# Attention through memory slots and a max-out FFN on one core: a new written-out order of the pieces behind the first 92

## The chip, the cores and the metric

The kernel runs on one core of one Trainium2 chip. A core has five engines that work side by side, each through its own instructions in order: TensorE (PE, with its weight loads PEld), VectorE (DVE), ScalarE (ACT), GpSimd (POOL) and SyncE (SP, which here only issues stores). They meet through semaphores. Tensors lie in SBUF, matmul results in the eight banks of PSUM, inputs and the output in HBM. The metric is the device time of one execution in microseconds (us), the median of several runs; lower is better.

## What is computed

For each of 8 batches, 8 heads and 576 positions, phi gives 32 memory slots whose softmax over the positions gathers keys and values; the queries attend to the 32 slots; the result goes through a max-out FFN.

```python
a = exp(phi - max(phi, axis=2)); a = a / sum(a, axis=2)      # over the 576 positions
k_m = einsum('bhsm,bhsd->bhmd', a, k); v_m = einsum('bhsm,bhsd->bhmd', a, v)
attn = softmax(q @ k_m.T / 8)                                # over the 32 slots
x = (attn @ v_m) as rows of 512                              # 8 heads x 64, 4608 rows
out = max(x @ w1, x @ w2, x @ w3) @ w_out                    # 512 -> 768 -> 512
```

## The kernel before

The kernel never forms `x`. It folds the memory values of a batch into the FFN's weights (`fold`, the D pieces), so that the attention weights `attn` multiply folded weights directly. The max over three products is taken as h = max(relu(x(w1-w3)), x(w2-w3)) plus a term x w3 that goes straight into the output product through w3 times w_out. So the first FFN stage has two weights for each of six column tiles of 128, and the second stage adds two matmuls on `attn` with the folded `wp3`.

The work is cut into 402 pieces, and a string near the end of the kernel (lines 758 to 785) writes out their order by hand. A word such as `F6@2` is piece F6 of batch 2; `issue` (line 722) emits all its instructions, in program order, to the engines that they need. There is no planner at run time: the order of the words is the order in each engine's queue, and each engine takes its own instructions strictly in that order. A mark `!` moves one instruction of the piece to another engine (an eviction from ScalarE to VectorE or back, a sum or copy between VectorE, ScalarE and GpSimd). A second string (lines 144 to 146) gives the PSUM banks in the order in which the pieces ask for them; a piece waits until the last reader of its bank is done.

The pieces that the text speaks of:

- L0 loads phi (`load_ph`, line 94), L1 and L2 load k and v into the raw buffers `kvo` (line 98), L3 loads q (line 113). All are issued from GpSimd's queue, which also carries computing; two buffers each.
- r0 and r1 (`pack`, lines 106 and 108) copy the loaded k and v of a batch into the packed buffer `kvr`, on GpSimd or, with the mark, on ScalarE. They free the raw buffer for the load two batches on.
- E (line 232) is the exponential of phi on ScalarE. B (line 250) gathers keys and values, 72 small matmuls. N (lines 270 to 285) normalises them on VectorE, K (line 300) transposes them on TensorE, with an eviction.
- Q0, Q1 (line 315) transpose q on VectorE. S (line 335) makes the scores, with two exponentials on ScalarE (line 344).
- The softmax of a batch, for its two halves 0 and 1: a (line 389, transpose), s (397, sum), c (406, reciprocal) on VectorE, m (411, multiplication) on GpSimd, X (419, transpose back into `attn`) on VectorE.
- D0 to D3 (line 442) fold the values into the weights, with an eviction of about 1 us.
- F0 to F11 (line 468) are the first FFN stage, four matmuls of 288 columns each; the even ones are evicted with a relu into `h1`, the odd ones by VectorE's max with `h1` into `hT` (line 481).
- T0 to T4 (lines 658 to 676) are the second FFN stage for 128 rows each, with an eviction and a store.
- Batches 5 and 6 do the second stage with seven block products in place of eight (P0 to P6, line 600), as Strassen's scheme does. Their sums of blocks are the pieces U (of weights) and A (of activations), all at line 505. These have two operands in SBUF and run on GpSimd or VectorE:

```python
def combine(on_dve, out_, in0, in1, op):
    eng = nc.vector if on_dve else nc.gpsimd
    eng.tensor_tensor(out=out_, in0=in0, in1=in1, op=op)
```

For U the mark `!` means VectorE, for A it means GpSimd.

The functions that matter for the change, with the line numbers of the profile:

Of the kernel before, what the change touches and what calls it, by code (L numbers as in the profile page):

```python
# [15 lines left out]
def kernel(  # L16
# [14 lines left out]
    B, H, S, D = q.shape  # L31
# [104 lines left out]
    for i in range(P // M):  # L136
# [4 lines left out]
    banks = iter(  # L141
        "".join(
            """
            00232204420145545045024602460260426042672643424260246024604260462342656204502406
            24062046204267240670462064260246024602064326247420640642064024620462042604605264
            620502645264034063460406064026042640246204203406767676
            """.split()
        )
    )
# [606 lines left out]


    for w in """
        E@0 H2@0 H0@0 L3@0 Z25@0 B0@0 Y2@0 I@0 N0@0 Z2@0 K0@0! Q0@0 Q1@0 Z9@0 S@0 Z2@0
        M0@0 M1@0 R0@0 R1@0 W0@0 Y3@0 W1@0 W2@0 Z6@0 O1@0 H3@0 O3@0 O2@0 H1@0 X1@0 B1@0  # L760
        X0@0 N1@0 K1@0 O0@0 Y0@0 D1@0! D0@0! D3@0 F8@0 F10@0 F2@0 V0@0 F6@0 F0@0! Y1@0
        D2@0 D4@0 F4@0 L0@1 V1@0 F1@0 E@1 F3@0 L1@1 F5@0 F9@0 F7@0 L3@1 F11@0 B0@1 T3@0
        N0@1 K0@1! L2@1 Q1@1 L2@2 L1@2 Q0@1 L0@2 V2@0 T0@0! L3@2 S@1 T1@0 a0@1 s0@1 c0@1
        m0@1 B1@1 N1@1 a1@1 L1@3 K1@1 s1@1 D0@1 D1@1! D2@1 c1@1 m1@1 X0@1 L3@3 r1@2 X1@1
        T2@0! L2@3 F6@1 F10@1 F7@1 F2@1 F3@1 F4@1 F0@1 r0@2 E@2 F5@1 F1@1 F11@1 L0@3
        L0@4 F8@1 L2@4 F9@1 B@2 D3@1 N@2 Q1@2 T0@1! K@2 T2@1! r0@3 Q0@2 S@2 a0@2 a1@2
        s1@2 c1@2 m1@2 T4@1! D1@2! s0@2 D2@2 c0@2 m0@2 X1@2 D0@2 T3@1 Q0@3 L3@4 X0@2
        Q1@3 T1@1 F0@2 F4@2 F8@2 F6@2 F9@2 E@3 F7@2 F1@2 L1@4 r1@3 F10@2 F2@2 L2@5 B@3
        N@3 D3@2 F3@2 L1@5 F5@2 K@3! U0@9 F11@2 S@3 U1@9 E@4 T3@2 L0@5 T0@2! a1@3 D1@3!
        s1@3 D2@3 a0@3 r1@4 c1@3 L3@5 D0@3 T1@2 m1@3 s0@3 Q0@4 X1@3 c0@3 m0@3 X0@3 T2@2!  # L770
        F4@3! r0@4 F5@3 L2@6 F0@3 D3@3 B@4 F6@3 N@4 F1@3 F8@3 Q1@4 F2@3 F9@3 K@4! F10@3
        r1@5 F7@3 S@4 F11@3 L3@6 D3@4 E@5 r0@5 F3@3 a0@4 U3@9 L0@6 a1@4 T4@3! L1@6 L0@7
        s1@4 D0@4 D1@4! B@5 c1@4 N@5 T1@3 Q1@5 K@5 L1@7 Q0@5 s0@4 c0@4 m0@4 T3@3! S@5
        a0@5 T2@3! s0@5 a1@5 c0@5 X0@4 m1@4 X1@4 D2@4 D0@5 D1@5 m0@5 s1@5 X0@5 T0@3!
        F4@4 c1@5 F2@4 m1@5 r1@6 L2@7 F10@4 r0@6 F3@4 F5@4 F8@4 X1@5 F9@4 F0@4 F11@4
        F6@4 E@6 F10@5! F7@4 L3@7 F0@5 F2@5 A4@5! Q0@6 A5@5! F1@4 F1@5 A7@5! F8@5 F6@5
        F4@5! Q1@6 D3@5 B@6 N@6 r0@7 D2@5 T0@4! F7@5 F5@5 K@6 F3@5 U2@9 F9@5 U0@5! T1@4!
        F11@5 A0@5 A6@5 r1@7! E@7 S@6 T2@4! D1@6! U1@5! D2@6 a0@6 Q1@7 B@7 A1@5! U2@5
        U3@5 N@7 T3@4 s0@6 K@7! Q0@7 a1@6 P1@5 D3@6 s1@6 c1@6 S@7 c0@6 A2@5! m1@6 P2@5
        P4@5 a0@7 s0@7 D3@7 D2@7 m0@6 a1@7 c0@7 D1@7! P0@5! A3@5! U0@6 s1@7 P5@5 c1@7  # L780
        m1@7 X1@6 X0@6 T4@5! D0@6! D0@7 P6@5 U1@6 m0@7 F8@6 F9@6 F6@6 U3@6 U2@6 X0@7
        P3@5 F10@6 F2@6 X1@7 F11@6 F8@7 F0@6 F3@6 F7@6 F4@7 F1@6 F9@7 F4@6 A4@6 F5@6
        F2@7 F0@7 F5@7 A0@6! A6@6! A1@6! F6@7 F10@7! F3@7 A5@6! P1@6 A2@6! F1@7 P0@6
        F7@7 A3@6! F11@7 P2@6! P4@6 T0@7 T1@7 P5@6! A7@6 T4@7 P6@6! P3@6! T2@7! T3@7
    """.split():
        n, b = w.rstrip("!").split("@")
        issue(int(b), n, w.endswith("!"))
# [30 lines left out]
```

## Time and profile before

| quantity | value |
|---|---|
| median of three runs | 163.83 us (163.65 to 164.19) |
| profiled execution, whole | 164.42 us |
| its span, first to last instruction | 162.4 us, 4946 instructions |
| TensorE busy | 152.6 us (94%), 2128 matmuls |
| VectorE busy | 104.5 us (64%) |
| ScalarE busy | 97.8 us (60%) |
| GpSimd busy | 92.2 us (57%) |
| loads on GpSimd's queue | 21.43 MB, 69.1% of 16 engines' span |
| stores on SyncE's queue | 9.90 MB, 17.3% |

Mean durations of the instructions that the text counts with, from the profile's groups: one F matmul 286 ns (they overlap), VectorE's max of an odd F 752 ns, ScalarE's relu 657 ns, eviction of a D piece 996 ns on ScalarE and 1211 on VectorE, the exponential of scores 653 ns each, transpose a 468 ns, sum s 740 ns, reciprocal c 246 ns, multiplication m 1154 ns, transpose X 456 ns, copy r 2111 ns, transpose Q 760 ns, a sum U or A on GpSimd 670 or 1640 ns by its size. A load of q, k or v takes 14 to 17 us from its issue to landing, because several are under way.

How to read a row of the timeline: start in us from the span's start, duration of the merged run of instructions, engine, line of the kernel, operation, output <- inputs, shapes, count, and in brackets the engine's idle time before it with what ended it. A row of the windows has the stretch, its length, and for PE, PEld, DVE, ACT and POOL the busy time and the instructions; then the granted clock, the DMA's busy share and GB/s. A busy TensorE isn't TensorE at its peak, since matmuls are pipelined; the starts of successive pieces tell more.

### The profile page before, as it was taken

What the parts mean: (1) busy time and instruction counts of PE and PEld (TensorE: products, weight loads), DVE (VectorE), ACT (ScalarE), POOL (GpSimd) and SP (SyncE); (2) the same over time, 40 slices, a digit from 0 to 9 for tenths busy, and PEclk for the clock granted to TensorE, in tenths of its full rate; (3) what the DMA queues carried; (4) which work ended last, traced back from release to release, by engine and by line L of the source; (5) the groups of instructions that cost most, each with busy time, mean ns of one, the idle gap of its engine ahead of it and who ended that gap; (6) DMA issues with size and microseconds to landing.
All of it is one profiled execution on the core that took longest, in us unless ns stands there. A gap on an engine that the chain in (4) does not pass through costs nothing.

```text
span 162.4 us, 4946 instructions
## 1 busy us (share of the span) xinstructions
PE 152.6 (94%) x2128; PEld 90.5 (56%) x2128; DVE 104.5 (64%) x201; ACT 97.8 (60%) x144; POOL 92.2 (57%) x92
## 2 busy tenths in 40 slices
PE   7958798999798999999999999999999999999991
PEld 2433544673366535753584536776456577785570
DVE  2013703898837847577487797986999967874340
ACT  4204535934497468977689849688779786631110
POOL 7931115100598359899877964999094880395000
PEclk9999999999999999999999999999999999999999
DMA  5999999999999999999999999999221044000365
GB/s 153 152 205 208 206 211 214 276 208 210 250 323 232 212 244 378 261 237 205 261 318 230 212 312 306 286 183 174 84 96 65 4 164 160 4 0 0 129 253 199
DMA packets 21909, 31.76 MB, mean 196 GB/s; under 512 B 1152, under 2 KB 16512, under 8 KB 21888
## 3 DMA queue, kind: packets, MB, share of 16 engines
q0 software_dynamic: 16080, 21.43, 69.1%
q1 hardware_dynamic: 5664, 9.90, 17.3%
q8 instruction: 16, 0.26, 0.6%
q10 hardware_dynamic: 144, 0.13, 0.2%
q14 instruction: 5, 0.04, 0.1%
HBM read 39.32 MB, written 9.44 MB: 300 GB/s over the span
## 4 chain that ended last, share of the span: by engine, by line
PE 62%; DMA 27%; DVE 4%; POOL 3%; ACT 1%; issue 1%; POOLq 0%
PE psum L468 22%; PE psum L658 17%; DMA ph<-in_phi_dram 15%; DMA w_sb<-in_moe_w_dram 12%; PE psum L600 8%; PE psum L667 5%; PE psum L442 4%; PE psum L250 2%; POOL kvo L98 2%; PE psum L676 1%; PE psum L335 1%; DVE twb L505 1%; PE psum L699 1%; ACT e L232 1%; PE psum L300 1%
## 5 line engine op out<-in xcount | busy, mean ns | idle before, releaser
L468 PE MATMUL psum<-attn,wp 128*128 128x288 bf16 x384 | 50.2, 286 | 0.2
L468 PEld LDWEIGHTS <-wp 128*128 128x128 bf16 x384 | 36.9, 98 | 12.0 <-issue 1.5
L481 DVE TENSOR_TENSOR hT<-psum,h 128x576 bf16<-128x576 f32 x48 | 34.5, 752 | 12.7 <-PE psum L468 8.3
L658 PE MATMUL psum<-wo_sb,hT 128*128 128x512 bf16 x162 | 39.6, 380 | 0.0
L173 ACT ACTIVATE h<-psum 128x576 bf16<-128x576 f32 x43 | 26.1, 657 | 7.2 <-PE psum L468 7.1
L175 ACT CAST wp<-psum 128x1024 bf16<-128x1024 f32 (+1 forms) x30 | 28.4, 996 | 2.6 <-PE psum L442 2.6
L175 ACT COPY ot<-psum 128x512 f32<-128x512 f32 x23 | 13.6, 591 | 23.2 <-PE psum L667 18.2
L411 POOL TENSOR_TENSOR t<-t,sm 128x576 bf16<-128x576 bf16 x14 | 16.1, 1154 | 19.2 <-DVE sm L406 19.2
L108 POOL COPY kvr<-kvo 128x2304 bf16<-128x2304 bf16 x11 | 23.2, 2111 | 5.5 <-DMA kvo<-in_k_dram 4.4
L658 PEld LDWEIGHTS <-hT 128*128 128x128 bf16 x162 | 14.6, 98 | 17.8 <-issue 3.2
L667 PE MATMUL psum<-wp,attn 128*128 128x512 bf16 x46 | 13.7, 379 | 0.0
L344 ACT ACTIVATE e<-psum 128x576 bf16<-128x576 f32 x16 | 9.6, 653 | 6.1 <-PE psum L335 6.1
L162 PE MATMUL psum<-warm 128*128 128x512 bf16 x44 | 12.1, 428 | 1.2 <-DVE warm L131 1.2
L315 DVE STREAM_TRANSPOSE qT<-qq 128x576 f32<-128x576 f32 x16 | 12.0, 760 | 1.1 <-DMA qq<-in_q_dram 1.0
L232 ACT ACTIVATE e<-ph 128x1152 bf16<-128x1152 f32 (+1 forms) x9 | 9.5, 1061 | 2.9 <-DMA ph<-in_phi_dram 2.7
L98 POOL DMA_DIRECT2D kvo<-in_v_dram x9 | 6.8, 753 | 7.4 <-PE psum L250 4.1
L397 DVE TENSOR_REDUCE sm<-t 128x18 f32<-128x576 bf16 x14 | 10.4, 740 | 0.2
L113 POOL DMA_DIRECT2D qq<-in_q_dram x8 | 6.1, 759 | 6.3 <-DMA w_sb<-in_moe_w_dram 6.0
L250 PEld LDWEIGHTS <-e 64*32 64x32 bf16 x720 | 7.1, 90 | 4.5 <-issue 2.8
L389 DVE STREAM_TRANSPOSE t<-e 128x288 f32<-128x288 f32 x14 | 6.5, 468 | 4.0 <-ACT e L344 4.0
L98 POOL DMA_DIRECT2D kvo<-in_k_dram x9 | 6.9, 769 | 2.9 <-DMA qq<-in_q_dram 2.1
L419 DVE STREAM_TRANSPOSE attn<-t 128x288 f32<-128x288 f32 x14 | 6.2, 456 | 3.5 <-POOL t L411 3.5
(94 smaller groups left out, 181.0 us busy)
## 6 DMA issues: line engine op xcount, KB each, us to landing
out_dram<-ot SPq DMA_DIRECT2D x27, 256.0 KB, 6.0
qq<-in_q_dram POOLq DMA_DIRECT2D x8, 576.0 KB, 14.0
ph<-in_phi_dram POOLq DMA_DIRECT2D x7, 576.0 KB, 16.0
kvo<-in_k_dram POOLq DMA_DIRECT2D x7, 576.0 KB, 15.9
kvo<-in_v_dram POOLq DMA_DIRECT2D x7, 576.0 KB, 16.7
w_sb<-in_moe_w_dram POOLq DMA_DIRECT2D x3, 768.0 KB, 19.4
out_dram<-oj SPq DMA_DIRECT2D x4, 512.0 KB, 2.8
wo_sb<-in_moe_w_out_dram POOLq DMA_DIRECT2D x1, 768.0 KB, 15.0
```

The lines of the kernel that those rows point to most:

```text
L98: nc.gpsimd.dma_start(out=kv[:, i, h].rearrange("p j c d -> p j (c d)"), in_=by_pair((k, v)[i], b)[:, h],)
L108: nc.gpsimd.tensor_copy(out=out_, in_=in_)
L162: nc.tensor.matmul(po[:, 0:BANK], lhsT=warm[:, 0:P], rhs=warm, start=True, stop=True)
L173: nc.scalar.activation(out=out_, in_=in_, func=AF.Relu)
L175: nc.scalar.copy(out=out_, in_=in_)
L315: nc.vector.transpose(out=s["qT"][:, j].rearrange("p j c r e -> p (j c r e)").bitcast(FP32), in_=loaded[b]["q"][:, j].rearrange("p j c d - ...
L411: (nc.vector if swap else nc.gpsimd).tensor_tensor(out=t, in0=t, in1=s["sm", g].unsqueeze(2).to_broadcast([P, S // HP, R, 2]), op=ALU.mult,)
L468: nc.tensor.matmul(acc[:, h, 0:SH], lhsT=wps[b][:, g, w * DF + ft * P : w * DF + (ft + 1) * P], rhs=attn[:, g, c0 : c0 + SH], start=(g == ...
L481: nc.vector.tensor_tensor(out=hT[:, ft, (b % 2) * S : (b % 2 + 1) * S].rearrange("p (h n) -> p h n", h=2), in0=a, in1=s["h1", ft], op=ALU.max,
L600: nc.tensor.matmul(po[:, q * CH : (q + 1) * CH], lhsT=lhs(k, q), rhs=rhs(k), start=(i < 3 and k == 0 and q == 0), stop=(k == KT and q == 1 ...
L658: nc.tensor.matmul(po, lhsT=hT[:, fc, c0 : c0 + P], rhs=wo_sb[:, fc, :], start=(n == 0), stop=False,)
L667: nc.tensor.matmul(po, lhsT=attn[:, g, c0 : c0 + P], rhs=wp3s[b][:, g, :], start=False, stop=(g == NG - 1),)
```

## The change

Only the two strings change. The first 92 words of the order (to `X0@1`) and the first 60 banks stay. All other words are put in a new order: the same 402 pieces, so the same matmuls, loads, copies and stores, but other places in each engine's queue. 42 of them change the mark, so that an instruction of theirs changes engine. Behind the 92, VectorE gets 161 instructions (155 before), ScalarE 101 (110) and GpSimd 48 (45, loads not counted). Of the sums at line 505, VectorE had U0@5, A0@5, A6@5, U1@5, A4@6 and A7@6; it now has U2@9, U3@6, A7@6 and A2@6. The copy r1@7 moves from ScalarE to GpSimd.

```diff
--- before.py
+++ after.py
@@ -141,9 +141,9 @@
     banks = iter(
         "".join(
             """
-            00232204420145545045024602460260426042672643424260246024604260462342656204502406
-            24062046204267240670462064260246024602064326247420640642064024620462042604605264
-            620502645264034063460406064026042640246204203406767676
+            00232204420145545045024602460260426042672643424260246024604206420142656204502460
+            42642064024606421042064026420620426050624265042124604204624062406204602460246206
+            241042616202641064216416462624264206240642604304101323
             """.split()
         )
     )
@@ -761,27 +761,27 @@
         X0@0 N1@0 K1@0 O0@0 Y0@0 D1@0! D0@0! D3@0 F8@0 F10@0 F2@0 V0@0 F6@0 F0@0! Y1@0
         D2@0 D4@0 F4@0 L0@1 V1@0 F1@0 E@1 F3@0 L1@1 F5@0 F9@0 F7@0 L3@1 F11@0 B0@1 T3@0
         N0@1 K0@1! L2@1 Q1@1 L2@2 L1@2 Q0@1 L0@2 V2@0 T0@0! L3@2 S@1 T1@0 a0@1 s0@1 c0@1
-        m0@1 B1@1 N1@1 a1@1 L1@3 K1@1 s1@1 D0@1 D1@1! D2@1 c1@1 m1@1 X0@1 L3@3 r1@2 X1@1
-        T2@0! L2@3 F6@1 F10@1 F7@1 F2@1 F3@1 F4@1 F0@1 r0@2 E@2 F5@1 F1@1 F11@1 L0@3
-        L0@4 F8@1 L2@4 F9@1 B@2 D3@1 N@2 Q1@2 T0@1! K@2 T2@1! r0@3 Q0@2 S@2 a0@2 a1@2
-        s1@2 c1@2 m1@2 T4@1! D1@2! s0@2 D2@2 c0@2 m0@2 X1@2 D0@2 T3@1 Q0@3 L3@4 X0@2
-        Q1@3 T1@1 F0@2 F4@2 F8@2 F6@2 F9@2 E@3 F7@2 F1@2 L1@4 r1@3 F10@2 F2@2 L2@5 B@3
-        N@3 D3@2 F3@2 L1@5 F5@2 K@3! U0@9 F11@2 S@3 U1@9 E@4 T3@2 L0@5 T0@2! a1@3 D1@3!
-        s1@3 D2@3 a0@3 r1@4 c1@3 L3@5 D0@3 T1@2 m1@3 s0@3 Q0@4 X1@3 c0@3 m0@3 X0@3 T2@2!
-        F4@3! r0@4 F5@3 L2@6 F0@3 D3@3 B@4 F6@3 N@4 F1@3 F8@3 Q1@4 F2@3 F9@3 K@4! F10@3
-        r1@5 F7@3 S@4 F11@3 L3@6 D3@4 E@5 r0@5 F3@3 a0@4 U3@9 L0@6 a1@4 T4@3! L1@6 L0@7
-        s1@4 D0@4 D1@4! B@5 c1@4 N@5 T1@3 Q1@5 K@5 L1@7 Q0@5 s0@4 c0@4 m0@4 T3@3! S@5
-        a0@5 T2@3! s0@5 a1@5 c0@5 X0@4 m1@4 X1@4 D2@4 D0@5 D1@5 m0@5 s1@5 X0@5 T0@3!
-        F4@4 c1@5 F2@4 m1@5 r1@6 L2@7 F10@4 r0@6 F3@4 F5@4 F8@4 X1@5 F9@4 F0@4 F11@4
-        F6@4 E@6 F10@5! F7@4 L3@7 F0@5 F2@5 A4@5! Q0@6 A5@5! F1@4 F1@5 A7@5! F8@5 F6@5
-        F4@5! Q1@6 D3@5 B@6 N@6 r0@7 D2@5 T0@4! F7@5 F5@5 K@6 F3@5 U2@9 F9@5 U0@5! T1@4!
-        F11@5 A0@5 A6@5 r1@7! E@7 S@6 T2@4! D1@6! U1@5! D2@6 a0@6 Q1@7 B@7 A1@5! U2@5
-        U3@5 N@7 T3@4 s0@6 K@7! Q0@7 a1@6 P1@5 D3@6 s1@6 c1@6 S@7 c0@6 A2@5! m1@6 P2@5
-        P4@5 a0@7 s0@7 D3@7 D2@7 m0@6 a1@7 c0@7 D1@7! P0@5! A3@5! U0@6 s1@7 P5@5 c1@7
-        m1@7 X1@6 X0@6 T4@5! D0@6! D0@7 P6@5 U1@6 m0@7 F8@6 F9@6 F6@6 U3@6 U2@6 X0@7
-        P3@5 F10@6 F2@6 X1@7 F11@6 F8@7 F0@6 F3@6 F7@6 F4@7 F1@6 F9@7 F4@6 A4@6 F5@6
-        F2@7 F0@7 F5@7 A0@6! A6@6! A1@6! F6@7 F10@7! F3@7 A5@6! P1@6 A2@6! F1@7 P0@6
-        F7@7 A3@6! F11@7 P2@6! P4@6 T0@7 T1@7 P5@6! A7@6 T4@7 P6@6! P3@6! T2@7! T3@7
+        m0@1 B1@1 N1@1 a1@1 L1@3 K1@1 s1@1 D0@1 D1@1! D2@1 c1@1 m1@1 X0@1 T2@0! X1@1
+        F2@1 F10@1! F8@1! L2@3 F0@1! F9@1 F6@1 r1@2 F11@1 F4@1 r0@2 F3@1 F1@1 L0@3 F7@1
+        E@2 L3@3 L1@4 F5@1 B@2 D3@1 N@2 U2@9! Q1@2 Q0@2 T1@1! K@2! T3@1 r0@3 S@2 a0@2
+        s0@2 L2@4 r1@3 a1@2 c0@2 s1@2 m0@2 T4@1 c1@2 D3@2 D1@2! D0@2 m1@2 X0@2 E@3 T0@1
+        T2@1! D2@2 B@3 X1@2 F6@2 N@3 F2@2 Q0@3 L0@4 F7@2 K@3! L3@4 F10@2 F8@2 Q1@3 L1@5
+        F3@2 F9@2 L2@5 F0@2 F11@2 F4@2 L0@5 F1@2 F5@2 L3@5 S@3 T3@2 a0@3 a1@3 s0@3 s1@3
+        c1@3 r0@4 c0@3 r1@4 D1@3! D0@3! m0@3 m1@3 L2@6 E@4 D2@3! X0@3 U0@9 U1@9 T2@2!
+        X1@3 T0@2! D3@3 B@4 N@4 F2@3 F4@3 F0@3 Q0@4 F8@3! F6@3 F9@3 F1@3 L0@6 K@4! r0@5
+        Q1@4 F10@3 F7@3 F11@3 F5@3 T1@2! S@4 F3@3 a0@4 E@5 T2@3 r1@5 D3@4 L1@6 a1@4 D2@4
+        B@5 T0@3! N@5 L2@7 D0@4 Q0@5 D1@4! U3@9 s0@4 Q1@5 K@5 L0@7 s1@4 T1@3 S@5 c0@4
+        c1@4 T3@3 L1@7 D0@5 a0@5 s0@5 m1@4 m0@4 a1@5 c0@5 X1@4 D1@5! X0@4 D3@5 s1@5 m0@5
+        T4@3 c1@5 F2@4 F10@4 r1@6 X0@5 F3@4 F6@4 F8@4 F7@4 L3@6 E@6 F11@4 F4@4 m1@5 r0@6
+        X1@5 r1@7 L3@7 F0@4 F9@4 A4@5! F5@4 F6@5 D2@5 B@6 F8@5 N@6 F10@5 U0@5 F9@5 r0@7
+        F2@5 F1@4 K@6! F3@5 F11@5 F0@5 E@7 F7@5 F4@5 F5@5 Q1@6 T2@4 D1@6! D0@6 B@7 T1@4
+        N@7 Q0@6 K@7! U2@5 Q0@7 F1@5 S@6 T0@4! U1@5 Q1@7 A5@5! a1@6 a0@6 S@7 a0@7 s0@6
+        T4@5! c0@6 A0@5! A1@5! A7@5! D3@6 A6@5! D0@7 U3@5 D3@7! s1@6 c1@6 m0@6 m1@6 a1@7
+        s1@7 T3@4 X1@6 P1@5 A2@5! X0@6 c1@7 D1@7! D2@7 D2@6 P2@5 m1@7 P4@5! F8@6 F0@6
+        s0@7 c0@7 P0@5! F2@6! P5@5 F6@6 F7@6 m0@7 F4@6 X0@7 U0@6 A4@6! X1@7 P6@5 F3@6
+        F9@6 A3@5! A5@6! F2@7! P3@5! U2@6 F10@6 F1@6 F11@6 F8@7 F4@7 A6@6! F5@6 F3@7
+        F6@7 F0@7! A0@6! F10@7! F9@7 P1@6 F7@7 F1@7 F11@7 P0@6! P2@6 F5@7 A1@6! U1@6
+        P4@6 A3@6! T4@7 U3@6! A7@6 A2@6 T0@7! P3@6! P5@6 T1@7 P6@6 T2@7! T3@7
     """.split():
         n, b = w.rstrip("!").split("@")
         issue(int(b), n, w.endswith("!"))
```

## The prediction, made before the changed kernel ran

> **What bounds the kernel now.** I read four views: the page's head, the busy time by window, the timeline by engine, and the DMA rows (single loads with their landing, and the packets of each queue). The first fence holds the page's head and one window, from the first matmul of the first moved tensor piece (T2@0) to that of the last piece (T3@7).
>
> ```profile
> span 162.4 us, 4946 instructions
> ...
> 44.28:157.08 112.80, 112.16 (x1498) 69.48 (x1491) 82.54 (x156) 77.33 (x111) 76.64 (x66) 1.00 0.79 189
> ```
>
> In those 112.80 us TensorE is busy for 112.16, at full clock; VectorE, ScalarE and GpSimd are each busy for 77 to 83. TensorE is the bound, the block products are the same, and a new order can only win what TensorE waits. Busy time hides short waits (matmuls overlap), so I went by starts, from TensorE's rows of the timeline (the first row is ScalarE's).
>
> ```profile
> 51.36 1.16 ACT L232 ACTIVATE e<-ph 128x1152 bf16<-128x1152 f32 x1 [1.01 <-DMA ph<-in_phi_dram]
> 52.58 0.80 PE L250 MATMUL psum<-kvr,e 64*32 64x129 bf16 x72 [0.52 <-ACT e L232]
> 57.26 0.47 PE L335 MATMUL psum<-qT,kvt 32*32 32x288 bf16 x32
> 61.70 0.59 PE L667 MATMUL psum<-wp,attn 128*128 128x512 bf16 x2
> 62.13 1.46 PE L658 MATMUL psum<-wo_sb,hT 128*128 128x512 bf16 x6
> 63.43 0.59 PE L667 MATMUL psum<-wp,attn 128*128 128x512 bf16 x2
> 63.93 0.53 PE L468 MATMUL psum<-attn,wp 128*128 128x288 bf16 x3
> 70.39 0.33 PE L300 MATMUL psum<-ident,kvn 128*128 128x128 bf16 x3
> 70.56 0.65 PE L468 MATMUL psum<-attn,wp 128*128 128x288 bf16 x4
> 71.28 0.48 PE L335 MATMUL psum<-qT,kvt 32*32 32x288 bf16 x32
> 79.06 0.59 PE L667 MATMUL psum<-wp,attn 128*128 128x512 bf16 x2
> 79.61 0.65 PE L468 MATMUL psum<-attn,wp 128*128 128x288 bf16 x4
> 89.67 0.63 PE L442 MATMUL psum<-w_sb,kvt 64*32 64x512 bf16 x16
> 90.11 0.83 PE L250 MATMUL psum<-kvr,e 64*32 64x129 bf16 x72
> 90.87 0.39 PE L658 MATMUL psum<-wo_sb,hT 128*128 128x512 bf16 x1
> 115.58 0.65 PE L468 MATMUL psum<-attn,wp 128*128 128x288 bf16 x4
> 116.16 0.47 PE L335 MATMUL psum<-qT,kvt 32*32 32x288 bf16 x32
> 121.34 0.55 PE L300 MATMUL psum<-ident,kvn 128*128 128x128 bf16 x3
> 121.72 0.49 PE L600 MATMUL psum<-wo_sb,hT 128*128 128x256 bf16 x3
> ```
>
> An F piece to an S piece takes 0.58 us where nothing is late (115.58 to 116.16), but 0.72 at S@3 (70.56 to 71.28): 0.14 lost. A K piece takes 0.17 (70.39 to 70.56), K@7 0.38 (121.34 to 121.72): 0.21. The last two matmuls of a T piece take 0.43 (61.70 to 62.13), but 0.50 ahead of F0@2 (63.43 to 63.93) and 0.55 ahead of F4@3 (79.06 to 79.61): 0.07 and 0.12. The largest wait, 0.52 at B@2, stands on a load: the exponential E@2 (51.36) started when phi of batch 2 had landed, and B@2 behind it.
>
> **The change part by part.** *What is kept.* The first 92 pieces and the issue of that phi load are untouched, and ahead of B@2 stand T2@0 and the same twelve F pieces in both orders. B@2 stays at 52.58 and its 0.52 stays. The end of the order is P6@6, T2@7, T3@7 where it was P3@6, T2@7, T3@7, so the output queue ends alike: 0.
>
> *What can be won.* The four small waits: 0.14 + 0.21 + 0.07 + 0.12 = 0.54 us. TensorE also pays some 0.09 (0.58 against 0.49 for an F piece) at a switch between whole and partial tiles; of these the new order has 39, the old 41, but five B pieces, not three, are followed by a whole tile. I take 0, between -0.19 and +0.1.
>
> *The two-operand instructions.* They stand on VectorE at L505. This fence is VectorE's and GpSimd's timeline around the one case where they met.
>
> ```profile
> 115.41 0.28 DVE L505 TENSOR_TENSOR twb<-wp 128x256 bf16<-128x256 bf16 x1
> 117.81 1.64 POOL L505 TENSOR_TENSOR w_sb<-w_sb,hT 128x768 bf16<-128x768 bf16 x1 [4.52 <-DVE w_sb L505]
> 117.84 1.75 DVE L505 TENSOR_TENSOR twb<-wp,twb 128x256 bf16<-128x256 bf16 x1
> ```
>
> U1@5 needs 0.28 us like its sister at 115.41, but takes 1.75 and ends 0.14 behind GpSimd's 1.64: 1.47 us of VectorE lost. What it cost TensorE is K@7's 0.21, since N@7 stood behind it on VectorE; the rest was hidden. The new order has four such instructions (U2@9, U3@6, A7@6, A2@6) for six. At U2@9 (about 55 us) GpSimd waits for a load, and at the other three (about 149 us) its last combination, A3@6, is over: no cost, and the gain is inside the 0.54.
>
> *The order on GpSimd, which is where I expect the price.* Its timeline in the old order, then the landing of the loads issued at 45.60 (q of batch 3) and 48.45 (v), each from the row of its line.
>
> ```profile
> 45.60 0.81 POOL L113 DMA_DIRECT2D qq<-in_q_dram  x1
> 48.45 0.74 POOL L98 DMA_DIRECT2D kvo<-in_v_dram  x1
> 57.64 2.11 POOL L108 COPY kvr<-kvo 128x2304 bf16<-128x2304 bf16 x1 [3.31 <-DMA kvo<-in_k_dram]
> 61.09 2.27 POOL L411 TENSOR_TENSOR t<-t,sm 128x576 bf16<-128x576 bf16 x2 [1.34 <-DVE sm L406]
> 65.17 2.10 POOL L108 COPY kvr<-kvo 128x2304 bf16<-128x2304 bf16 x1 [0.32 <-DMA kvo<-in_v_dram]
> 63.40 0.48 DVE L419 STREAM_TRANSPOSE attn<-t 128x288 f32<-128x288 f32 x1
> ...
> DMA to landing us min/median/max: 15.3/15.3/15.3
> DMA to landing us min/median/max: 16.7/16.7/16.7
> ```
>
> The loads land in order of issue: k of batch 3 at 57.6, which ends the wait of r0@3 (57.64), q at 60.9, v at 65.1: slots of 3.3 and 4.2 us. In the old order the multiplications m1@2 and m0@2 (61.09) stood ahead of r1@3, the copy that waits for v of batch 3 (65.17). In the new one L2@4 and r1@3 stand ahead of m0@2 and m1@2, and v is issued right behind k. Queued behind the waiting r1@3 on GpSimd are m0@2 and m1@2, behind them on VectorE X0@2, T0@1's eviction and X1@2, and on TensorE F6@2.
>
> The sum: v takes q's slot and lands at 60.9; r1@3 60.95 to 63.06; the two multiplications 2.27, to 65.28; X1@2 0.48, to 65.8; F6@2's third matmul, which reads X1@2's half, at 65.85. Without a wait it would start at 65.15: S@2 at 57.2 as before; S, T4, three D and two T took 6.6 us (57.26 to 63.93, less 0.07); one D more is 0.22 (two from 89.67 to 90.11), B 0.76 (90.11 to 90.87), one switch more 0.09, two matmuls 0.25. Price 0.68. The lower end is 0.23: r1@3 can't start ahead of 60.45, when r0@3 (57.64 + 2.11) and L2@4 (0.74) are through. The upper end goes by v's own 4.2 us: 61.8, so 1.6. I take 0.68, the slot of a load of the same size at the same place.
>
> Outputs decide which slot it is. The rows below are the DMA answers for 54 to 58 us (the loads' queue, and the one output issued then) and for 60 to 64 us.
>
> ```profile
> q0 software_dynamic: 730, 0.81, 119.7%
> out_dram<-ot SPq DMA_DIRECT2D x1, 256.0 KB, 6.5
> ...
> q0 software_dynamic: 346, 1.03, 75.3%
> q1 hardware_dynamic: 253, 0.46, 31.8%
> ```
>
> With outputs (q1) in flight the loads move 346 packets in 4 us, without them 730. In the new order the outputs of T1@1 and T3@1 are issued at about 57.3 and 58.0, inside v's slot. Were they served at once, v would move at half speed from 58 on and land near 62. The old order's output, issued at 56.13, had no packet by 58.0 (54 to 58 lists no q1), so by this row they begin near 60 and v keeps the short slot.
>
> The Trainium skill ("DMA: Bandwidth & Descriptors", section "Queues, rings and completion order") says that a DMA engine takes turns between the rings that have work, a packet at a time; by that they would be served at once, and the sum would be the first rival's. The trace agrees with the sharing and not with its early start.
>
> *The next load, behind this.* The load of phi of batch 5, and E@5, which reads it:
>
> ```profile
> L94 POOL DMA_DIRECT2D ph<-in_phi_dram x1: 787/787/787, 72.4 to 72.4; - x1
> DMA to landing us min/median/max: 16.1/16.1/16.1
> ...
> 88.50 1.16 ACT L232 ACTIVATE e<-ph 128x1152 bf16<-128x1152 f32 x1
> ```
>
> E@5 started as its load landed (72.4 + 16.1 = 88.5). The same set of loads goes ahead of it in the new order, so E@5 again ends near 89.66. But B@5 (90.11) comes earlier: from S@2 TensorE needed 90.11 - 57.26 - 0.33 of waits = 32.5 us; the new order has a T4 and a D less and, net, no other piece changed save one T more (-0.4): 89.3. So B@5 would wait 0.4 if F6@2 hadn't; with the 0.68 it is covered. Each covers the other, so no less than 0.4 of the 0.54 is given back.
>
> *VectorE's queue.* Three evictions of F in a row on its timeline:
>
> ```profile
> 66.65 2.09 DVE L481 TENSOR_TENSOR hT<-psum,h 128x576 bf16<-128x576 f32 x3 [2.11 <-PE psum L468]
> ```
>
> They take 0.7 us each; TensorE makes an F in 0.49. Where a bank comes back after 1.47 to 1.64 us (F1@2 to T3@2, F9@3 to F7@3, F9@5 to F3@5, F2@5 among them) I find 0 to 0.1 us of room; I charge 0.18 in all, between 0 and 0.7 (one eviction late).
>
> Sum: -0.54 + 0 + 0.68 + 0.18 = +0.32 us. The profiled execution had 162.4 us of span and 164.42 in all, 0.59 above the runs' median of 163.83. I put the 0.32 on that median: 164.15, in the profiled terms 162.7 and 164.7.
>
> **The rivals.** *Loads come late (slower).* The outputs take half the DMA from 58 on, v lands near 62, F6@2 loses 1.7 us, and the copy r1@4, again ahead of m0@3 and m1@3, may repeat it at F2@3: 163.83 - 0.54 + 1.7 + 0.18 = 165.2. It decides from a landing of 61.1 on, where the sum passes +0.5. For it speaks v's 4.2 us slot; against it, the output that began late. It is also what the page's rule gives. *VectorE falls behind (slower).* D0@3 and D2@3 are evicted on VectorE between S@3 and X0@3. By the means in the table above, S@3's start to X1@3's end is 1.8 for the exponentials, 0.5 for the second transpose, 1.5 for two sums, 0.5 for two reciprocals, 2.4 for the evictions and 0.9 for two X: 7.6 us. The matmul that needs it stands 7.8 behind S@3 (three T 5.2, four D 0.9, B 0.8, S 0.4, two matmuls 0.25, switches 0.2). One eviction more (0.67) and a bank late elsewhere give +0.9: 164.7. *A real gain (faster).* If v lands by 60.4 and E@5's load by 88.1, the waits are 0.23 and no more: 163.83 - 0.54 + 0.23 - 0.19 = 163.3. Against it stands E@5's row. *It doesn't do what it says:* if U2@9 meets a GpSimd copy it takes up to 2.1 us, and S@2, with 0.7 of room, loses 1.4: 165.5. GpSimd's 3.31 us wait at that place speaks against it.
>
> **How the numbers follow.** Forecast 0.50, loads late 0.27, VectorE behind 0.10, not as said 0.05, real gain 0.08. 0.3% of 163.83 is 0.49 us, about what a measurement of this kernel can tell. So faster 0.08, same 0.50, slower 0.42. The forecast's own range is 163.7 to 164.4 (prices 0.4 to 0.9); the range of 8 in 10 goes up to the late loads, 163.5 to 165.2.
>
> **What would show it.** Right: GpSimd idle ahead of L108 at about 59.7, ended by v's load; F6@2 about 65.6, 0.7 behind its place; K@7 back at 0.17; all L505 on VectorE at 0.28 or 0.56. Wrong: F6@2 without a wait, B@5 ahead of 89.6, a TensorE wait of more than 0.4 at a place not named here, or an output tail that isn't like the old one.

## The result and the profile after

The new order takes 163.26 us (median of 20 runs, 162.47 to 163.93) where the old one takes 163.81 (median of 20 beside them, 163.01 to 164.72). The ratio is 0.9965, with a 95% interval of 0.9949 to 0.998: faster by 0.55 us, where a loss of 0.32 us had been forecast. From the page of the profiled execution (163.93 us in all, 164.42 before), its head and its busy times:

```profile
span 161.9 us, 4956 instructions
...
PE 152.6 (94%) x2128; PEld 90.5 (56%) x2128; DVE 108.5 (67%) x207; ACT 91.2 (56%) x135; POOL 94.5 (58%) x95
```

TensorE's 152.6 us are those of before; only its waits can have changed. To find them I use a stretch that begins behind B@2's wait: from B@2's first matmul to T3@7's. Its row in the windows (stretch, length, then busy time and instructions of PE, PEld, DVE, ACT, POOL), first of the changed kernel, then of the kernel before in a second profile (`before_again`, below):

```profile
52.64:156.64 104.00, 103.97 (x1436) 64.15 (x1436) 80.91 (x153) 64.69 (x94) 71.45 (x63) 1.00 0.76 184
```

```profile
52.42:156.90 104.48, 104.33 (x1436) 64.09 (x1436) 78.12 (x149) 69.93 (x101) 69.20 (x60) 1.00 0.76 182
```

104.00 against 104.48, at the same clock (1.00) and for the same 1436 matmuls. The tail behind the stretch, to the span's end, took 5.3 us in all seven profiles of the two kernels. So 0.48 us lie between B@2 and T3@7, though VectorE has 2.8 us more to do there. TensorE's timeline in the changed kernel at the places that the prediction spoke of:

```profile
52.64 0.80 PE L250 MATMUL psum<-kvr,e 64*32 64x129 bf16 x72
64.24 0.83 PE L250 MATMUL psum<-kvr,e 64*32 64x129 bf16 x72
65.00 1.64 PE L468 MATMUL psum<-attn,wp 128*128 128x288 bf16 x12
71.15 0.47 PE L335 MATMUL psum<-qT,kvt 32*32 32x288 bf16 x32
71.65 1.46 PE L658 MATMUL psum<-wo_sb,hT 128*128 128x512 bf16 x6
89.35 0.83 PE L250 MATMUL psum<-kvr,e 64*32 64x129 bf16 x72
116.76 0.33 PE L300 MATMUL psum<-ident,kvn 128*128 128x128 bf16 x3
116.93 0.65 PE L468 MATMUL psum<-attn,wp 128*128 128x288 bf16 x4
```

B@2 has no wait in brackets. From B@3 to F6@2 are 0.76 us, a B piece's normal length: the 0.68 that was to be paid at F6@2 is not there. B@5 starts at 89.35, where TensorE's own work puts it. K@7 lasts 0.17. The one wait that I find behind B@2 is at T3@2: 0.50 behind S@3, which takes 0.42 where nothing is late, so 0.08.

The chain that was to carry the price, on GpSimd and VectorE of the same timeline (two rows of copies, r0@3 and r1@3; then m0@2 and m1@2 in one row; X0@2 and X1@2):

```profile
56.92 2.11 POOL L108 COPY kvr<-kvo 128x2304 bf16<-128x2304 bf16 x1 [3.51 <-DMA kvo<-in_k_dram]
59.78 2.11 POOL L108 COPY kvr<-kvo 128x2304 bf16<-128x2304 bf16 x1
61.85 2.27 POOL L411 TENSOR_TENSOR t<-t,sm 128x576 bf16<-128x576 bf16 x2
63.04 0.48 DVE L419 STREAM_TRANSPOSE attn<-t 128x288 f32<-128x288 f32 x1 [1.18 <-POOL t L411]
64.16 0.48 DVE L419 STREAM_TRANSPOSE attn<-t 128x288 f32<-128x288 f32 x1
...
DMA to landing us min/median/max: 13.5/13.5/13.5
```

The chain itself is as forecast, link by link: r1@3 as soon as v lands, the multiplications behind it, X1@2 behind them. But it is early. The last row is the answer for v's load, issued at 46.2 and landed 13.5 later, at 59.7 and not at 60.9; X1@2 ends at 64.64, and F6@2's third matmul reads it at about 65.25 (65.00 and two matmuls), 0.6 later.

### The profile page after: what moved, and what is told of

Read it like the earlier page. It is cut to its first block, busy times and chain, and to the rows that moved or that the text cites. A ratio compares the mean times of both kernels' runs of the same rounds, so it can differ in the third digit from the quotient of the medians.

```text
span 161.9 us, 4956 instructions
## 1 busy us (share of the span) xinstructions
PE 152.6 (94%) x2128; PEld 90.5 (56%) x2128; DVE 108.5 (67%) x207; ACT 91.2 (56%) x135; POOL 94.5 (58%) x95
## 4 chain that ended last, share of the span: by engine, by line
PE 78%; DMA 14%; POOL 4%; issue 1%; DVE 1%; ACT 0%; DVEq 0%; POOLq 0%
PE psum L468 28%; PE psum L658 23%; DMA w_sb<-in_moe_w_dram 14%; PE psum L600 8%; PE psum L667 6%; PE psum L442 5%; PE psum L250 3%; PE psum L335 2%; POOL kvo L98 2%; PE psum L676 1%; POOL w_sb L119 1%; PE psum L699 1%; PE psum L300 1%; POOL qq L113 0%; POOL wo_sb L126 0%
## 5 line engine op out<-in xcount | busy, mean ns | idle before, releaser
L175 ACT CAST wp<-psum 128x1024 bf16<-128x1024 f32 (+1 forms) x29 | 27.3, 992 | 6.5 <-PE psum L442 6.4
L173 ACT ACTIVATE h<-psum 128x576 bf16<-128x576 f32 x39 | 24.1, 656 | 11.6 <-PE psum L468 11.1
L108 POOL COPY kvr<-kvo 128x2304 bf16<-128x2304 bf16 x12 | 25.2, 2108 | 6.7 <-DMA kvo<-in_k_dram 4.7
L175 ACT COPY ot<-psum 128x512 f32<-128x512 f32 x19 | 11.2, 587 | 18.9 <-PE psum L667 15.9
L162 PE MATMUL psum<-warm 128*128 128x512 bf16 x44 | 12.6, 440 | 1.2 <-DVE warm L131 1.2
L442 PE MATMUL psum<-w_sb,kvt 64*32 64x512 bf16 (+1 forms) x200 | 7.9, 372 | 1.3 <-DMA w_sb<-in_moe_w_dram 1.0
```

Source lines behind the costliest of these rows:

```text
L108: nc.gpsimd.tensor_copy(out=out_, in_=in_)
L162: nc.tensor.matmul(po[:, 0:BANK], lhsT=warm[:, 0:P], rhs=warm, start=True, stop=True)
L173: nc.scalar.activation(out=out_, in_=in_, func=AF.Relu)
L175: nc.scalar.copy(out=out_, in_=in_)
L442: nc.tensor.matmul(ps[M * j : M * (j + 1), a, 0 : hi - lo], lhsT=lhs[r, M * j : M * (j + 1)], rhs=rhs[r, j, :], start=(i == 0), stop=(i == ...
```

## The experiments

What separates the theories: the gain may be (A) the small waits of TensorE in the old order, each with its own cause; (B) the meeting of VectorE's two-operand instruction with GpSimd's alone; (C) B@2's wait for its load. The forecast price may be (P) real and dependent on when the loads land, or (R) worth nothing in any case. P' is the counterpart of P: that the early copy costs nothing because the new order needs it early, for B@3.

**The two kernels again.** No edit: three more profiles of the old order and two more of the new one.

> The kernel before, unchanged, for a second profile. Theory A (the gain is the four small waits at F0@2, S@3, F4@3 and K@7): the same four waits, 0.07 + 0.14 + 0.11 + 0.21 us within 0.1 in sum, whatever the phase of the loads. Theory C (the gain is the 0.5 us wait at B@2, which the profile of the changed kernel hasn't): the wait at B@2 is there again at 0.5, and in no profile of the changed order. If A is right the wait at B@2 changes from profile to profile with the landing of phi of batch 2 and the start of T2@0, in either kernel.

> The changed kernel, unchanged, for a second profile. A: no wait over 0.1 us behind B@2; from B@2 to T3@7 104.0 us (104.5 in the kernel before). k of batch 3 lands between 56.5 and 58, v of batch 3 some 2.9 us behind it, and F6@2 has no wait as long as X1@2 ends ahead of 65.2. C: a difference in B@2's wait again, at 0.5.

> The kernel before, unchanged, for the landing of phi of batch 2. In three of five profiles with the old order it landed 3.0 us behind k of batch 2 and B@2 waited 0.4 to 0.6, in two 1.5 us behind it and B@2 didn't wait; with the new order 1.5 to 2.1 in all five and no wait. If the late landing belongs to the old order (C in part): late here in more than half of the profiles. If it is chance and belongs to neither (A alone): late in old and new alike, in some three of ten.

> The changed kernel, unchanged. C in part: phi of batch 2 lands 1.5 to 2.1 us behind k again, no wait at B@2. A alone: as likely late as in the old order. Either way 104.0 us from B@2 to T3@7.

> As before_b. Either way 104.4 to 104.6 us from B@2 to T3@7, with the waits at S@3 (0.14) and K@7 (0.21).

Measured from B@2 to T3@7: 104.50 in the profile that I predicted from, 104.48, 104.47 and 104.39 in the three further ones of the old order; 104.00, 104.03 and 104.16 in the new one. The means, 104.46 and 104.06, differ by 0.40, and no old profile is below a new one. Single times were 164.11, 163.64 and 163.19 against 162.94 and 163.46, so one execution says little, while this stretch repeats to 0.16 or better. TensorE's timeline of `before_again`, with GpSimd's r0@3 from its other rows:

```profile
52.42 0.79 PE L250 MATMUL psum<-kvr,e 64*32 64x129 bf16 x71
56.48 2.12 POOL L108 COPY kvr<-kvo 128x2304 bf16<-128x2304 bf16 x1 [2.54 <-DMA kvo<-in_k_dram]
70.40 0.65 PE L468 MATMUL psum<-attn,wp 128*128 128x288 bf16 x4
71.12 0.49 PE L335 MATMUL psum<-qT,kvt 32*32 32x288 bf16 x32
86.58 0.41 PE L442 MATMUL psum<-w3o,kvt 64*32 64x512 bf16 x8
87.03 0.66 PE L468 MATMUL psum<-attn,wp 128*128 128x288 bf16 x4
121.15 0.54 PE L300 MATMUL psum<-ident,kvn 128*128 128x128 bf16 x3
121.53 0.71 PE L600 MATMUL psum<-wo_sb,hT 128*128 128x256 bf16 x5
```

S@3's 0.14 (0.72 for 0.58) and K@7's 0.21 (0.38 for 0.17) are here again, and in the other two. B@2 doesn't wait: C falls as the cause of this difference, since its wait was absent from all three further profiles of the old order while the stretch behind it stayed long. F4@3's 0.12 is gone too; instead F3@3 waits 0.11 (0.45 behind D3@4, 0.34 in the profile that I predicted from; 0.12 and 0.04 in the other two). F0@2's is 0.05 to 0.07 in all. So the old order waits 0.14 + 0.21 + 0.05 and 0.04 to 0.12, that is 0.44 to 0.52, and the new one 0.08: a difference of 0.36 to 0.44, beside the 0.40 measured. That speaks for A.

What S@3 waits for stands in the answer on the waits of TensorE's weight loads in the profile that I predicted from (what waited and what ended it: us in total, times, longest):

```profile
PEld L335 <- ACT kvt L175: 0.4, 1, 0.4
```

It is K@3's eviction on ScalarE: one F piece stands between K@3 and S@3 in the old order, nine in the new one. F0@2 and F4@3 start 0.05 to 0.06 behind the end of X0@2 and of X0@3 on VectorE (63.88 and 79.55), which they read. For F3@3 I found no cause in the rows.

The same profiles show what I had not looked for: the loads stand differently against TensorE from execution to execution. Between B@2's start and r0@3's (k of batch 3 has landed) are 5.06 us in the profile that I predicted from (52.58 to 57.64), 4.06 in `before_again` (52.42 to 56.48), 4.53 and 4.43 in `before_b` and `before_c`, 4.28 in the first of the new order.

In `after_b` they are 5.0, and here the price shows. Its timeline on TensorE, GpSimd and VectorE, with B@2 at 52.08:

```profile
57.08 2.11 POOL L108 COPY kvr<-kvo 128x2304 bf16<-128x2304 bf16 x1 [3.40 <-DMA kvo<-in_k_dram]
...
63.68 0.83 PE L250 MATMUL psum<-kvr,e 64*32 64x129 bf16 x72
64.31 0.48 DVE L419 STREAM_TRANSPOSE attn<-t 128x288 f32<-128x288 f32 x1
64.45 1.78 PE L468 MATMUL psum<-attn,wp 128*128 128x288 bf16 x12
```

X1@2 ends at 64.79, where F6@2's third matmul was due at 64.70 (64.45 and two matmuls), and the twelve F matmuls take 1.78 instead of 1.64: 0.14 lost, which is the surplus of this profile's stretch (104.16 against 104.00 and 104.03). P, not R. With each profile's waits taken off its stretch (0.54, 0.51, 0.52 and 0.44 in the old order, 0.08, 0.08 and 0.22 in the new one), 103.92 to 103.97 us are left in all seven: the waits are the whole difference in the stretch.

**Half of each order.** `new_then_old` has the new order's first 254 words, then the missing pieces in the old order's sequence; `old_then_new` the old order's first 252 words, then the rest as the new one has it. The seam of the first, against the new order:

```diff
...
-        T4@3 c1@5 F2@4 F10@4 r1@6 X0@5 F3@4 F6@4 F8@4 F7@4 L3@6 E@6 F11@4 F4@4 m1@5 r0@6
+        T4@3 c1@5 L3@6 X0@5 F4@4 F2@4 m1@5 r1@6 F10@4 r0@6 F3@4 F5@4 F8@4 X1@5 F9@4 F0@4
...
```

> The new order up to T4@3, c1@5 (254 words), then the remaining pieces in the old order. A: the early three waits (F0@2, S@3, F4@3) are gone, K@7's 0.21 is back: 0.3 us faster than before. B (the gain is the collision of U1@5 on VectorE with GpSimd alone): no faster than before, since U1@5 is on VectorE again beside GpSimd. Wherever the two orders don't join well, a wait shows at the seam and is told apart by its place.

> The old order up to X0@5, T0@3 (252 words), then the remaining pieces in the new order. A: the early waits stay (0.32 us), K@7's 0.21 is gone: 0.2 us faster than before. B: 0.5 us faster, all of the gain.

171.19 us, ratio 1.0436 (1.0394 to 1.0478), and 168.48, ratio 1.0267 (1.0227 to 1.0307). Both pay at the seam, which the forecasts underrated. TensorE's timeline, first of `new_then_old` (the F piece at the seam, then K@7 with what follows it), then of `old_then_new` (the B piece at the seam):

```profile
112.44 1.12 PE L468 MATMUL psum<-attn,wp 128*128 128x288 bf16 x4 [4.93 <-DVE hT L481]
128.44 0.50 PE L300 MATMUL psum<-ident,kvn 128*128 128x128 bf16 x3
128.78 0.82 PE L600 MATMUL psum<-wo_sb,hT 128*128 128x256 bf16 x6
```

```profile
117.47 1.18 PE L250 MATMUL psum<-kvr,e 64*32 64x129 bf16 x72 [2.37 <-POOL kvr L108]
```

An F piece waits 4.93 us for VectorE, a B piece 2.37 for a copy on GpSimd: the pieces next to the seam were prepared by neither order. The waits aren't the whole of it: behind them the granted clock was 0.50 from 112.4 to 118.0 in `new_then_old` (the six matmuls of a T piece took 2.74 us there and 1.46 later) and 0.67 on average from 117.4 to 122.0 in `old_then_new`. As times these runs tell nothing of the halves. But the waits go with the halves: with the old second half K@7 lasts 0.34, 0.17 too long, and S@3 has no wait; with the old first half S@3 waits its 0.14, and K@7 takes 0.16 in the new second half. Each wait has a cause of its own, as A has it.

**The meeting of VectorE and GpSimd, taken away from the old order.** U1@5 runs on GpSimd:

```diff
-        F11@5 A0@5 A6@5 r1@7! E@7 S@6 T2@4! D1@6! U1@5! D2@6 a0@6 Q1@7 B@7 A1@5! U2@5
+        F11@5 A0@5 A6@5 r1@7! E@7 S@6 T2@4! D1@6! U1@5 D2@6 a0@6 Q1@7 B@7 A1@5! U2@5
```

> The kernel before with one mark changed: U1@5 on GpSimd, its place kept. A: the collision is gone, N@7 comes 0.8 us earlier and K@7's wait of 0.21 goes, all other waits stay; from B@2 to T3@7 104.25 us (104.47 and 104.51 in the two profiles of before), so 0.2 us faster. B (the collision alone is the gain): 0.5 us faster and 104.0 from B@2 to T3@7.

163.63 against 163.83 (29 runs), ratio 0.9982 (0.9959 to 1.0004): of the size expected, but no time that differs for certain. The stretch from B@2 to T3@7 took 104.60 us in its profile, where A had 104.25 and B 104.0: both missed. The loads were late in it (r0@3 5.07 behind B@2), and two other waits were longer, 0.24 at F4@3 and 0.20 at F3@3, where the four profiles of the kernel before have 0.04 to 0.12 for the two together. The places of the waits are clearer. Timeline of `u1_gpsimd`:

```profile
115.83 0.67 POOL L505 TENSOR_TENSOR twb<-wp,twb 128x256 bf16<-128x256 bf16 x1 [2.54 <-DVE twb L505]
119.72 0.17 DVE L270 RECIPROCAL rden<-psum 128x2 f32<-128x2 f32 x1 [0.75 <-PE psum L250]
121.33 0.33 PE L300 MATMUL psum<-ident,kvn 128*128 128x128 bf16 x3
121.50 0.82 PE L600 MATMUL psum<-wo_sb,hT 128*128 128x256 bf16 x6
```

U1@5 takes 0.67 on GpSimd, N@7's reciprocal waits for TensorE and no longer for VectorE's queue, and K@7 lasts 0.17: its 0.21 is the meeting's, as the prediction had it. S@3's 0.14 and F0@2's 0.07 are still there, some 50 us ahead of the meeting, and the new order hasn't them, so B is too narrow.

**The meeting, put into the new order.** U1@5 and U2@5 on VectorE, where GpSimd is at its own sums:

```diff
-        N@7 Q0@6 K@7! U2@5 Q0@7 F1@5 S@6 T0@4! U1@5 Q1@7 A5@5! a1@6 a0@6 S@7 a0@7 s0@6
+        N@7 Q0@6 K@7! Q0@7 F1@5 S@6 T0@4! Q1@7 A5@5! a1@6 U1@5! a0@6 U2@5! S@7 a0@7 s0@6
```

> The changed kernel with U1@5 and U2@5 on VectorE behind a1@6 and a0@6, where GpSimd runs A0@5 and A1@5: the collision that the change avoids, put in twice. The two need 0.28 us each on a free port. If they stall to the end of GpSimd's instruction they take 0.5 to 2 us each, 1.2 to 3.3 together. A (what TensorE loses is the delay less the room behind it): F8@6 is due 0.9 us behind X0@6's end, so TensorE waits 0.3 to 2.4 there. B' (VectorE has so much room that it never shows): no wait on TensorE over 0.1.

163.04, ratio to before 0.9965 (0.9938 to 0.9993): as the changed kernel itself. VectorE and GpSimd in its timeline:

```profile
117.56 1.64 POOL L505 TENSOR_TENSOR w_sb<-hT 128x768 bf16<-128x768 bf16 x1 [6.32 <-DVE hT L481]
118.83 0.53 DVE L505 TENSOR_TENSOR twb<-wp,twb 128x256 bf16<-128x256 bf16 x1
119.29 1.64 POOL L505 TENSOR_TENSOR w_sb<-w_sb,hT 128x768 bf16<-128x768 bf16 x1
119.68 1.39 DVE L505 TENSOR_TENSOR twb<-wp 128x256 bf16<-128x256 bf16 x1
120.99 0.47 DVE L389 STREAM_TRANSPOSE t<-e 128x288 f32<-128x288 f32 x1
```

Both meetings happened: 0.53 and 1.39 for instructions that need 0.28, each ending 0.14 to 0.16 behind GpSimd's instruction, as U1@5 did in the old order. They took 1.36 us from VectorE and nothing from TensorE (104.01 from B@2 to T3@7). VectorE had room: the transpose behind them starts 69.26 us behind B@2 (51.73 in this profile), in the changed kernel 68.41 behind it, so 0.85 later, and what reads it could wait as long. The wait of 0.3 to 2.4 that A had here didn't come; B' held.

**The copy r1@3 early in the old order.** L2@4 and r1@3 ahead of m1@2, with L2@3 early enough for it:

```diff
-        ... X0@1 L3@3 r1@2 X1@1 T2@0! L2@3 F6@1 ... L0@4 F8@1 L2@4 F9@1 ... c1@2 m1@2 ... F1@2 L1@4 r1@3 F10@2
+        ... X0@1 L2@3 L3@3 r1@2 X1@1 T2@0! F6@1 ... L0@4 F8@1 F9@1 ... c1@2 L2@4 r1@3 m1@2 ... F1@2 L1@4 F10@2
```

> The kernel before with GpSimd's order around r1@3 as in the new order: L2@3 ahead of L3@3, and L2@4 and r1@3 ahead of m1@2. With k of batch 3 landing 4.2 us behind B@2, as in four of five profiles: r0@3 from 56.65, L2@4, r1@3 59.6 to 61.7, the multiplications to 64.0, X0@2 to 64.5, where F0@2 is due at 63.75. P (the price that I forecast is real, and the new order hides it by putting D3@2 and B@3, 0.98 us, ahead of F6@2): F0@2 waits 0.7 (up to 1.5 in a profile whose loads are late). R (the copy ahead of the multiplications costs nothing anywhere): no more wait at F0@2 than before, 0.0 to 0.1.

165.41, ratio 1.0105 (1.0061 to 1.0149). The timeline of GpSimd, VectorE and TensorE around F0@2, in a profile whose loads were late (r0@3 5.07 behind B@2):

```profile
60.76 2.11 POOL L108 COPY kvr<-kvo 128x2304 bf16<-128x2304 bf16 x1 [0.52 <-DMA kvo<-in_v_dram]
62.83 2.27 POOL L411 TENSOR_TENSOR t<-t,sm 128x576 bf16<-128x576 bf16 x2
64.94 0.78 DVE L315 STREAM_TRANSPOSE qT<-qq 128x576 f32<-128x576 f32 x1 [0.44 <-DMA qq<-in_q_dram]
65.64 0.44 DVE L419 STREAM_TRANSPOSE attn<-t 128x288 f32<-128x288 f32 x1
66.13 0.65 PE L468 MATMUL psum<-attn,wp 128*128 128x288 bf16 x4 [2.30 <-DVE attn L419]
```

The price is real: the copy holds the multiplications, and TensorE waits 2.30 at F0@2 for the transpose at line 419. About 0.5 of it has a second cause that I had not named: q now lands behind v, and Q0@3, which waits for it, stands ahead of X0@2 on VectorE (X0@2 could have run at 65.10, when the multiplications ended, and ran at 65.64). The other 1.8 I put down to the copy; it is more than the 1.5 that I had allowed for late loads.

**The load of v later in the new order.** L2@3 behind L0@3, the copy where it was:

```diff
-        F2@1 F10@1! F8@1! L2@3 F0@1! F9@1 F6@1 r1@2 F11@1 F4@1 r0@2 F3@1 F1@1 L0@3 F7@1
+        F2@1 F10@1! F8@1! F0@1! F9@1 F6@1 r1@2 F11@1 F4@1 r0@2 F3@1 F1@1 L0@3 L2@3 F7@1
```

> The changed kernel with one load moved: L2@3 (v of batch 3) is issued behind L0@3, not ahead of it, so that v lands one phi load, some 1.6 us, later. P: X1@2 ends about 4.9 us behind v's landing, near 66.1 (B@2 at 52.4), where F6@2 needs it at 65.05: a wait of 1.0 us at F6@2, and 0.9 to 1.1 us slower than the changed kernel, so slower than before by 0.4. R: hidden, as fast as the changed kernel.

164.12, ratio to before 1.0011 (0.9983 to 1.0039): 0.86 above the changed kernel, with v landing at 60.60. The same chain in its timeline:

```profile
60.65 2.11 POOL L108 COPY kvr<-kvo 128x2304 bf16<-128x2304 bf16 x1 [1.39 <-DMA kvo<-in_v_dram]
63.78 0.83 PE L250 MATMUL psum<-kvr,e 64*32 64x129 bf16 x72
65.02 1.80 PE L468 MATMUL psum<-attn,wp 128*128 128x288 bf16 x11 [0.41 <-DVE ot L179]
65.03 0.48 DVE L419 STREAM_TRANSPOSE attn<-t 128x288 f32<-128x288 f32 x1
```

F6@2 starts 1.24 behind B@3 instead of 0.76 (its bank waits for T0@1's eviction, which stands between X0@2 and X1@2 on VectorE), and its matmuls take 0.3 more for X1@2: 0.78 in all, the price that the prediction named, at the place that it named, from a landing as late as it assumed (8.4 us behind B@2, 8.3 in the prediction).

**The multiplications ahead of the copy in the new order.**

```diff
-        s0@2 L2@4 r1@3 a1@2 c0@2 s1@2 m0@2 T4@1 c1@2 D3@2 D1@2! D0@2 m1@2 X0@2 E@3 T0@1
+        s0@2 a1@2 c0@2 s1@2 m0@2 T4@1 c1@2 D3@2 D1@2! D0@2 m1@2 L2@4 r1@3 X0@2 E@3 T0@1
```

> The changed kernel with L2@4 and r1@3 behind m0@2 and m1@2 on GpSimd, as in the old order: the step that I priced, undone alone. P' (the new order needs the copy early, since it has B@3 ahead of F6@2): the multiplications end near 63.0, L2@4 63.8, r1@3 65.9, and B@3, due at 64.1 with B@2 at 52.4, waits some 1.8 us: 1.5 to 1.9 us slower than the changed kernel. P (as forecast, the early copy costs 0.2 to 0.7 at F6@2): faster than the changed kernel by that. R (the place is free): as fast as the changed kernel.

164.90, ratio to before 1.0057 (1.0028 to 1.0086), and 1.64 above the changed kernel. Its timeline:

```profile
63.36 2.12 POOL L108 COPY kvr<-kvo 128x2304 bf16<-128x2304 bf16 x1
65.53 0.80 PE L250 MATMUL psum<-kvr,e 64*32 64x129 bf16 x72 [1.58 <-POOL kvr L108]
```

B@3 reads that copy and stands ahead of F6@2 in the new order. It starts at 65.53 where it was due at 63.76, 1.77 late (1.8 was expected; the row's 1.58 is the idle time that shows beside the matmul ahead of it). P' holds: the early copy isn't a price paid for nothing; without it the new order would be slower than the old.

## Why the prediction was wrong, step by step

**The 0.68 at F6@2: the step that failed.** The mechanism was right in each link: a landing at 60.6 produced it (`new_v_late`, 0.78), a late execution of the changed kernel showed a trace of it (`after_b`, 0.14). Wrong was the landing of v at 60.9, on which the rest of the sum stands, because two figures of one execution were taken as fixed. First, k at 57.6 was the landing of one execution whose loads were late: 5.06 behind B@2, against 4.06 to 4.53 in the other three of the old order. Second, v's slot behind k was taken as q's, 3.3; it measured 2.9 (56.86 to 59.73). In the changed kernel v landed at 59.73 instead of 60.9, and X1@2 was 0.6 early instead of 0.65 late. The lower end that I gave, 0.23, was built on the same late k, so the range had no end for a normal execution.

**The cover at B@5, "no less than 0.4 of the 0.54 is given back": failed too, for another reason.** B@5 came where it was forecast (89.3, measured 89.35), but phi of batch 5 was to land at 88.5 as before, since the same set of loads goes ahead of it. In the changed kernel, the answer for the loads of phi issued at 64.1 and 67.1, and E@5 on ScalarE:

```profile
DMA to landing us min/median/max: 10.8/15.4/19.9
...
87.83 1.17 ACT L232 ACTIVATE e<-ph 128x1152 bf16<-128x1152 f32 x1
```

The second landed at 87.0, and E@5 ended at 89.0, ahead of B@5's 89.35. Against B@2 it is 34.3 us, 35.9 before; the old order's other profiles have 36.1 to 36.2 and the new one's 34.3 to 35.4, so about 1 of it belongs to the new order and isn't the late execution's. By the DMA rows up to this landing the stores' queue had moved 3.74 MB in the changed kernel and 4.00 before, one store of 256 KB fewer; that may be the reason, and I didn't try it. "The same set of loads goes ahead" was true and not enough.

**What can be won, 0.54: right in size, one entry wrong.** The old order's other three profiles give 0.44 to 0.52. It is no ceiling: in `u1_gpsimd`, without K@7's 0.21, the other waits came to 0.65. S@3, K@7 and F0@2 were steady; F4@3's 0.12 is absent from the three further profiles of the old order, whose loads weren't late (0.24 in `u1_gpsimd`, whose r0@3 stood 5.07 behind B@2), and F3@3's 0.04 to 0.12 was absent from the one that I predicted from.

**B@2's wait "stays": wrong as a statement of the order.** It stayed in none of the new order's profiles, and was absent from three of the old order's four.

**The meeting on VectorE: right.** It cost K@7's 0.21, and I find no other wait of TensorE behind it. In the new order VectorE's four instructions at line 505 meet nothing: each takes 0.28 or 0.55. The first, U2@9, in VectorE's timeline of the changed kernel:

```profile
54.93 0.55 DVE L505 TENSOR_TENSOR w3T<-wo_sb 128x768 bf16<-128x768 bf16 x1
```

**VectorE's queue, 0.18: right place, half the size.** T3@2 waits 0.08 for the bank of F1@2, one of those named. **Switches and tail at 0: right.** Without its waits the stretch is as long in both orders (103.92 to 103.97), and the tail took 5.3 us in both.

**The rivals.** The real gain (0.08) came, 163.3 forecast and 163.26 measured, by its own condition: v by 60.4 (59.73) and E@5's load by 88.1 (87.0). That the times agree so well is luck in part: of its terms the 0.23 came as 0.08 and the -0.19 for switches as nothing, and of the medians' 0.55 only 0.40 is found in the stretch. VectorE falling behind came as T3@2's 0.08 alone, and U2@9 met no copy. Loads late didn't come. Two stores were issued from 57.4 on, inside v's slot; the DMA rows of the changed kernel for 54 to 62 us:

```profile
q0 software_dynamic: 1250, 1.82, 108.5%
q1 hardware_dynamic: 97, 0.20, 7.3%
```

In eight microseconds the stores' queue (q1) moved 0.20 MB, less than one store, and v's slot was 2.9 us. The Trainium skill ("DMA: Bandwidth & Descriptors", section "Queues, rings and completion order") says that a DMA engine takes turns between rings that have work; by the prediction's estimate that would have put v near 62, if the stores had work from their issue on. They begin late, as the prediction read from the old order: the answer for 57.4 to 60 us lists no packet of q1 at all, and v had landed by then. "Half speed" was a misreading besides. The 730 and 346 packets that the prediction set against each other are of different sizes; in bytes the loads moved 0.81 MB in 4 us without stores and 1.03 MB with them.

**What stays open.** Why the loads stand up to 1 us differently against TensorE isn't settled; the instructions up to there are the same in both orders. The semaphore events in the traces narrow it down. A load's landing is sixteen events. For k of batch 3 fifteen of them had come by 55.65 to 56.10 us in all fourteen profiles; the last came 0.05 to 1.87 behind them: 1.87 in the profile that I predicted from, 0.68 in `before_again`, 1.21 in the first profile of the new order. So one part of sixteen sets a load's landing, in either order, and what delays it is open. The same lag explains the slot of 3.3: fifteen events of q came 2.9 behind those of k, and the last one lagged by 2.3 instead of 1.87. Phi of batch 2 landed 3 us behind k, and B@2 waited, in three of the seven profiles that begin with the old order (the one that I predicted from, `u1_gpsimd` and `old_r1_early`), and never in the seven that begin with the new one; whether that is chance or the old order's doing, and so whether B@2's wait adds to the 0.40 in the medians' 0.55 (0.33 to 0.84 by the interval), these runs don't tell.

## What to carry to other kernels

A landing time is a sample, not a property of the kernel: take it against the bottleneck engine's own place, in several profiles, and where a price or a wait is shorter than the spread (here about 1 us), price it at both ends and let the nearer end be nothing. A shift on GpSimd or VectorE costs only what the queue behind it lacks in room: the same meeting cost 0.21 in one place and nothing in another. And an operation that is moved ahead of others has to be asked who needs it early, as well as whom it holds.

## What the hardware showed that I had not expected

With the same instructions ahead of it, k of batch 3 landed 4.0 to 5.0 us behind B@2's start, and phi of batch 2 either about 1.5 to 2.1 or 3.0 us behind k; TensorE's stretch of 104 us behind it repeated to 0.16 or better in the profiles of either kernel. So two profiles of one kernel may show waits at different places (F4@3 or F3@3) with nearly the same sum.

A store that is issued while its queue is empty starts late as long as loads are moving. In the packets of the changed kernel's trace the stores issued at 57.43, 74.19 and 87.00 moved their first packet 3.44 to 3.49 us later; behind the last load the delay was 0.83 to 0.89 (stores issued from 115.1 on).
